# Carving setup scratch out of residual buffers, and rebalancing the setup engines, in a four-layer SSM/convolution kernel

## Chip, cores, metric

The kernel runs on one core of one Trainium2 chip. The metric is the device time of one execution in microseconds (us); lower is better. Engines are named as the profile names them: PE (TensorE, matrix products), PEld (its weight loads), DVE (VectorE), ACT (ScalarE), POOL (GpSimd), SP (SyncE, which issues most of the DMAs here).

The timings of one kernel spread by 1 to 2% with the granted TensorE clock. A few runs (one of `after_w3`, one each of `merged_w4`, `merged_late_w4` and `arena_late_w3`) are marked slow. The ratios leave these runs out; the medians quoted are of all runs, and differences are taken from the ratios. The rounds of experiments ran on different chips, each together with the kernel before, which is another reason to compare by ratio. Stage times are each read from one profiled execution, so a stage difference of a few us is not resolved by them.

## The reference, cut to what matters

```python
# x: [1, 2048, 640].  Four layers, each after a layernorm, each added to x:
x = x + A(layernorm(x))      # state-space layer: h_t = Lam_bar*h_{t-1} + B_bar x_t ; y = 2 Re(C h) + D x
x = x + Bl(layernorm(x))     # y = q * longconv(v * shiftconv(k)), q = layernorm(x)
x = x + A(layernorm(x))      # same weights again
x = x + Bl(layernorm(x))
# in Bl: k_shift = 4-tap causal convolution of k; kv = k_shift * v
#        y = irfft(rfft(kv, 4096) * rfft(ssm_k, 4096))[:2048] + kv * ssm_D
```

The long convolution doesn't depend on `x`. The kernel computes it once, as a side stream beside the first SSM layer, and both B layers only multiply by the result.

## The kernel before

The rows of `x` are cut into 16 chunks of 128. Each engine has its own instruction list; a scheduler lays out the lists when the kernel is built, so the order on an engine can differ from the source's. The kernel has two phases.

**Phase one** is the first SSM layer of all chunks, in four interleaved streams, with the FFT convolution as side stream. A round takes `FFT_W` steps of the FFT and then one step of each SSM stream:

```python
FFT_W = 3
NS1, NS2 = 4, 5
EVAC_DVE_EVERY = dict(T=2, F1=0, F2=4, I2=3, I1=2)   # every n-th PSUM eviction of a stage goes to DVE, 0: all to ACT

def run_streams(streams, side=None, side_w=1000, steps_per_chunk=None):
    ...
    while any(alive) or side is not None:
        if side is not None:
            for _ in range(side_w):
                next(side)                 # (StopIteration handled: cut)
        for i in reversed(range(n)):
            if alive[i] and rnd >= i:
                next(streams[i])           # (cut)
        rnd += 1
```

**An SSM chunk** goes x → T (transpose) → U (product with B) → P (two elementwise products) → G (prefix sums and carry) → H → Y → `xres`:

```python
    psT = ps("T", [P, D], BF16)                                   # PE transposes, ACT evicts to xT
    ...
    psU = ps("U", [P, D2], F32)                                   # 15 matmuls, L213
    ...
    U = wk.tile([P, D2], BF16, name="U", tag="uh")
    nc.scalar.copy(out=U[:], in_=psU[:])                          # L215
    yield
    P01 = wk.tile([P, D2], BF16, name="P01", tag="pa"); P23 = wk.tile([P, D2], BF16, name="P23", tag="pb")
    nc.vector.tensor_mul(out=P01[:], in0=U[:], in1=K["Wm2"][:])   # L218
    nc.vector.tensor_mul(out=P23[:], in0=U[:], in1=K["Wm2s"][:])  # L219
    yield
    psG = ps("G", [P, NB + 2, P], F32)
    ...
        nc.vector.scalar_tensor_tensor(out=x_dst, in0=psY[:], ..., in1=resid, ...)   # L274, writes xres[k]
```

In phase one T, U and G of every chunk share **one** PSUM buffer, since the FFT holds three banks.

```python
            if nm == "G" and "G" in pools:            # only in phase two
                return pools["G"].tile(shape, dt, name="ps_G", tag="G")
            if nm in ("T", "U", "G"):
                return psU.tile(shape, dt, name="ps_" + nm, tag="U")     # bufs=1
```

The buffer goes from use to use in the order of PE's list. In the trace of the kernel before, the first uses are T of chunks 0 and 1, U of chunk 0 (88.8 us), T of 2, U of 1 (96.3), T of 3, U of 2 (106.5), and only then the first G (110.7). So a use whose input is late holds back all uses behind it, those of other chunks too. T needs the chunk's layernorm (`xb`, after short DVE operations), U needs T, and G needs P.

**The side stream** prepares XB (a 40 KB-per-partition array), then transforms it:

```python
    XB = xbp.tile([P, 16, 2, D], BF16, name="XB")
    TF1 = make_TF1(tc, xbp, T)                        # DFT table; its temporaries in a pool of its own
    ...
        for dt in range(NT):
            ks = kp.tile([P, S], BF16, name="ksm", tag="ksm")
            nc.sync.dma_start(out=ks[:], in_=B_ssm_k[dt * P:(dt + 1) * P, :])
            nc.vector.tensor_add(out=ks[:, 0:1], in0=ks[:, 0:1], in1=dD[:, dt:dt + 1])
            ...                                        # 16 transposes (L539), 4 evictions into XB ("T")
    ...
    nc.sync.dma_start(out=XB[:, :, 0, :], in_=kview)  # 2.6 MB
    nc.vector.memset(hal[0:1, :, :], 0.0)             # L550
    ...
            nc.vector.tensor_copy(out=wj[:, j, :], in_=wsh[:, :, j])     # L559, four of them
    ...                                                # 4-tap convolution on DVE: L580 (product), L582 (sum), L583 (times v)
    TI1 = make_TI1(tc, tip, T)                        # tables for the inverse transform
    make_CS(tc, env["fconst"], T)                     # sines and cosines
    ...                                                # F1 (L600): first DFT -> DRAM; F2, pointwise, I2 (L666) -> DRAM; I1 (L686) -> ybuf
```

**Phase two** is the other three layers, in nine streams, with its own PSUM buffer for G. It starts after both streams of phase one are through:

```python
        run_streams(g1, side=gf, side_w=FFT_W, steps_per_chunk=7)
    pools["G"] = ctx.enter_context(tc.tile_pool(name="psumG", bufs=1, space=PSUM))
    ...
    run_streams(gens, steps_per_chunk=8)
```

## Time and profile before

| | before |
|---|---|
| time, median of 3 runs (range) | 587.6 us (587.23 to 588.56) |
| span in the profile, mean granted clock | 586.2 us, 0.876 |
| PE / DVE / ACT busy | 417.0 / 414.0 / 336.0 us (71 / 71 / 57%) |
| transposes of the filter | 62 to 85 us |
| convolution on DVE | 88 to 164 us |
| first DFT (F1) done | 186.7 us |
| last DFT (I1) done | 391.9 us |
| last SSM chunk of phase one done | 394.8 us |
| first ps_U matmul of phase two | 411.0 us |

No engine is full on average, so the reading goes by stages. The first view is busy time by windows: each row is a stretch of the span in us, its length, the busy time and instruction count of each engine, the granted TensorE clock, the DMA share and GB/s.

```profile
...
core 0: us, PE busy (x) PEld busy (x) DVE busy (x) ACT busy (x) POOL busy (x), PEclk, DMA share, GB/s
...
30.00:60.00 30.00, 1.41 (x10) 0.91 (x10) 25.79 (x65) 7.34 (x12) 4.65 (x1) 0.50 0.30 91
60.00:90.00 30.00, 14.36 (x94) 10.46 (x95) 9.08 (x23) 7.25 (x12) 0.00 (x0) 0.50 0.31 101
90.00:120.00 30.00, 21.62 (x101) 9.66 (x100) 24.83 (x36) 17.60 (x34) 1.64 (x3) 0.84 0.32 113
...
390.00:420.00 30.00, 11.95 (x74) 6.39 (x73) 15.15 (x74) 24.88 (x54) 4.77 (x9) 0.72 0.21 72
...
```

PE has 1.41 us of work in 30 to 60, which is an empty setup; and in 390 to 420 again only 11.95 of 30. What PE waited for in the setup is seen from the transposes of the filter (one line's instructions: how many, their durations in ns, first and last start, then what ended the idle time before them):

```profile
...
L539 PE MATMUL ps_T<-identb,ksm x80: 265/314/314, 62.1 to 85.0; 128*128 128x128 bf16 x80
...
  DVE ksm L535: 13.2, 1
...
```

They could start only at 62.1, and the first of them waited for the filter's own load. The DMA issuer's waits between 40 and 65 us tell why that load was late:

```profile
...
SPq L549 <- DVE WmT L107: 22.9, 1, 22.9
SPq L531 <- DVE TF L484: 7.4, 1, 7.4
...
```

XB's load (L549) waited 22.9 us for a table computation (WmT), and the first load of the filter's stage (L531, just ahead of the filter's tiles L534 on the same queue) 7.4 us for the last write of the DFT table. Neither load needs the result that it waited for. They lay in the same SBUF bytes: the temporary pools had been closed and the new tiles took their place. Then follows the convolution (the products that start an accumulation),

```profile
...
L580 DVE TENSOR_TENSOR acc<-XB,wj x7: 483/818/824, 88.3 to 147.6; 128x1280 bf16<-128x1280 bf16 x6, 128x640 bf16<-128x640 bf16 x1
...
```

from 88.3 us on. At the other end, the timeline of PE shows the change of phase (start, duration, engine, line, operation; in brackets the idle time before it and its releaser):

```profile
...
394.46 0.22 PE L269 MATMUL ps_Y<-DS,xT 128*128 128x128 bf16 x1
405.62 0.71 PE L204 MATMUL ps_T<-identb,xb 128*128 128x128 bf16 x5 [10.94 <-ACT xb L200]
...
411.03 4.31 PE L213 MATMUL ps_U<-BT,xT 128*128 128x512 bf16 x15 [1.39 <-ACT xT L206]
```

After the last matmul of phase one (394.5) PE is idle for 11 us and the first useful product of phase two starts at 411.0. Both streams had ended almost together (391.9 and 394.8), so `ybuf` had to be reloaded and a B layer computed with nothing else to do.

### The profile page before, as it was taken

The page shows a single profiled execution, that of the slowest core. Times are in us where ns is not written, and L with a number is a line of the kernel's source. Part 1 is how long each engine was busy: PE and PEld are TensorE (multiplying, and loading weights), DVE is VectorE, ACT ScalarE, POOL GpSimd, SP SyncE. Part 2 cuts the span into 40 slices and gives each one's busy share as a digit, 9 for nine tenths or more (in the row PEclk, how much of TensorE's full clock was granted, in tenths as well). Part 3 has the DMA queues.
Part 4 walks back from the last instruction along what each step waited for, and adds up shares of the span by engine and source line. Part 5 has one row for each costly group of instructions (what it writes and reads, how often), then busy time and mean ns, then how long its engine had stood idle before and what let it go on. Part 6 is the DMA issues. An engine that isn't in the chain of part 4 may idle for free. (4 is left out here: it accounts for less than half of the span.)

```text
span 586.2 us, 7978 instructions
## 1 busy us (share of the span) xinstructions
PE 417.0 (71%) x2814; PEld 225.2 (38%) x2814; DVE 414.0 (71%) x1126; ACT 336.0 (57%) x583; POOL 40.2 (7%) x81
## 2 busy tenths in 40 slices
PE   3300357689774789779898975990679898989981
PEld 3300233334332345334444432550335554545540
DVE  3798136998996297666888653665566888896883
ACT  2640122865868435555645652567965788965552
POOL 4003000000010000000000000003000101100001
PEclk9655557978878899989999997995889999999997
DMA  7305321444522441664563228123000101010000
GB/s 256 104 0 178 124 83 27 181 158 172 210 102 73 118 102 38 143 142 107 122 152 96 68 67 358 79 104 101 1 1 1 46 25 46 23 34 12 23 24 35
DMA packets 26791, 54.76 MB, mean 93 GB/s; under 512 B 6143, under 2 KB 14847, under 8 KB 26494
## 3 DMA queue, kind: packets, MB, share of 16 engines
q1 hardware_dynamic: 23806, 43.76, 25.0%
q0 software_dynamic: 2944, 10.49, 5.7%
q8 instruction: 22, 0.36, 0.3%
q14 instruction: 19, 0.16, 0.1%
HBM read 33.26 MB, written 20.97 MB: 93 GB/s over the span
## 5 line engine op out<-in xcount | busy, mean ns | idle before, releaser
L213 PE MATMUL ps_U<-BT,xT 128*128 128x512 bf16 (+1 forms) x480 | 106.1, 375 | 20.3 <-ACT xT L206 19.5
L266 PE MATMUL ps_Y<-CT,H 128*128 128x128 bf16 (+1 forms) x640 | 107.9, 307 | 8.5 <-DVE xres L274 6.5
L213 PEld LDWEIGHTS <-xT 128*128 128x128 bf16 x480 | 49.6, 105 | 68.6 <-issue 38.3
L215 ACT CAST U<-ps_U 128x1280 bf16<-128x1280 f32 x32 | 39.1, 1222 | 58.5 <-PE ps_U L213 58.4
L266 PEld LDWEIGHTS <-H 128*128 128x128 bf16 x640 | 49.2, 99 | 44.1 <-issue 12.5
L238 ACT CAST G<-ps_G 128x1280 bf16<-128x1280 f32 x32 | 39.2, 1225 | 34.5 <-PE ps_G L236 27.5
L233 PE MATMUL ps_G<-Lpos,P 128*128 128x128 bf16 x320 | 47.2, 221 | 7.8 <-ACT U L215 6.3
L218 DVE TENSOR_TENSOR P<-U,Wm 128x1280 bf16<-128x1280 bf16 x32 | 26.3, 820 | 32.8 <-ACT U L215 32.8
L519 ACT CAST s<-ps_F 128x512 bf16<-128x512 f32 (+1 forms) x96 | 42.2, 553 | 7.7 <-PE ps_F L600 7.6
L175 ACT ACTIVATE ln_junk<-xres 128x640 bf16<-128x640 f32 x48 | 35.0, 730 | 13.2 <-DVE c L247 4.7
L519 ACT CAST XS<-ps_F 128x512 bf16<-128x512 f32 (+1 forms) x70 | 36.5, 578 | 5.5 <-PE ps_F L639 5.0
L233 PEld LDWEIGHTS <-P 128*128 128x128 bf16 x320 | 29.8, 97 | 19.0 <-issue 13.7
L600 PE MATMUL ps_F<-XB,TF 128*128 128x512 bf16 (+1 forms) x96 | 29.9, 376 | 10.0 <-ACT s L519 5.4
L204 PE MATMUL ps_T<-identb,xb 128*128 128x128 bf16 x160 | 15.5, 233 | 29.3 <-ACT xb L200 18.9
L234 PEld LDWEIGHTS <-P 128*128 128x128 bf16 x320 | 31.3, 98 | 10.0 <-issue 7.8
L206 ACT COPY xT<-ps_T 128x640 bf16<-128x640 bf16 x32 | 22.2, 694 | 17.9 <-PE ps_T L204 17.9
L638 PE MATMUL ps_F<-a2in,F_C 128*128 128x512 bf16 (+1 forms) x76 | 29.5, 388 | 3.4 <-DVE a2o L517 2.5
L236 PE MATMUL ps_G<-E,cT 20*128 20x512 bf16 (+1 forms) x90 | 31.4, 349 | 0.0
L285 ACT ACTIVATE bq<-xres,ln_nb,ln_rstd 128x640 bf16<-128x640 f32 x32 | 28.6, 916 | 4.2 <-DVE ln_nb L188 4.1
L539 PE MATMUL ps_T<-identb,ksm 128*128 128x128 bf16 x80 | 11.7, 302 | 24.7 <-DVE ksm L535 13.2
L219 DVE TENSOR_TENSOR P<-U,Wm2s 128x1280 bf16<-128x1280 bf16 x32 | 26.1, 815 | 0.4 <-ACT U L215 0.4
L255 DVE TENSOR_TENSOR M<-G,TA 128x1280 bf16<-128x1280 bf16 x32 | 26.1, 816 | 0.0
(256 smaller groups left out, 809.7 us busy)
## 6 DMA issues: line engine op xcount, KB each, us to landing
Ad<-s SPq DMA_DIRECT2D x32, 320.0 KB, 2.2
a2in<-Ad SPq DMA_DIRECT2D x28, 320.0 KB, 5.1
AIN<-ad SPq DMA_DIRECT2D x2, 2560.0 KB, 12.0
ad<-a2o SPq DMA_DIRECT2D x28, 160.0 KB, 2.6
xin<-in_A_x_dram POOLq DMA_DIRECT2D x16, 160.0 KB, 2.9
vb<-in_B_v_dram POOLq DMA_DIRECT2D x8, 320.0 KB, 3.3
XB<-in_B_k_dram SPq DMA_DIRECT2D x1, 2560.0 KB, 10.5
ksm<-in_B_ssm_k_dram SPq DMA_DIRECT2D x5, 512.0 KB, 3.4
```

The costliest lines, as they stand in the source:

```text
L175: nc.scalar.activation(out=junk[:], in_=x_ap, func=ACTF.Square, accum_out=ssq[:])
L213: nc.tensor.matmul(out=psU[:, c0:c1], lhsT=xT[:, dt * P:(dt + 1) * P], rhs=BTf[:, dt, c0:c1], start=dt == 0, stop=dt == NT - 1)
L215: nc.scalar.copy(out=U[:], in_=psU[:])
L233: nc.tensor.matmul(out=psG[:, b, :], lhsT=src[:, pt * P:(pt + 1) * P], rhs=Lpos[:], start=b == b0, stop=False)
L234: nc.tensor.matmul(out=psG[:, b, :], lhsT=src[:, D + pt * P:D + (pt + 1) * P], rhs=sgn[:], start=False, stop=lastmm)
L236: nc.tensor.matmul(out=psG[:, b0:b0 + nb_, :], lhsT=cT[:], rhs=K["E2"][:, b0:b0 + nb_, :], start=False, stop=True)
L238: nc.scalar.copy(out=G[:].rearrange("p r t j -> p (r t) j"), in_=psG[:, 0:NB, :])
L266: nc.tensor.matmul(out=psY[:, c0:c1], lhsT=H[:, hi, pt, :], rhs=CT[:, pt, hi, c0:c1], start=n == 0, stop=False)
L285: nc.scalar.activation(out=q[:], in_=x, func=ACTF.Identity, bias=nb[:, 0:1], scale=rstd[:, 0:1])
L519: nc.scalar.copy(out=out, in_=in_)
L600: nc.tensor.matmul(out=pt_[:, :c1 - c0], lhsT=TF1[:, r, mh, :], rhs=XBf[:, r, c0:c1], start=True, stop=True)
L638: nc.tensor.matmul(out=pt_[:, :c1 - c0], lhsT=C[:], rhs=a2f[:, ro, c0:c1], start=True, stop=False)
```

## The change

The intent: temporaries of the setup go into the tiles of the residual `xres`, which are written late (chunks 2 to 8 and 9 to 15), so that XB, the filter tiles and the inverse table no longer overlap them in memory. Weight loads use working tiles of the SSM streams. Some setup work moves from DVE to POOL, the evictions of the transposes all go to ACT, and the FFT gets four steps in a round in place of three.

```diff
+class Arena:                    # hands out pieces of one SBUF tile; release(mark) frees them
+    ...
-    es = ExitStack(); tp = es.enter_context(tc.tile_pool(name="tbl_tmp", bufs=1))
+                                # build_tables, fft_tables, make_CS, make_TF1, make_TI1 take an arena `tp` instead
 ...
-            w = wl.tile([P, NT, D], BF16, name="wsb", tag="wsb")
-            nc.sync.dma_start(out=w[:], in_=src.rearrange("(t p) d -> p t d", p=P))
+            for (t0, t1, tag) in parts:                      # ((0,2,"pa"), (2,4,"pb"), (4,NT,"uh"))
+                w = wk.tile([P, 2, D], BF16, name="wsb", tag=tag)
+                nc.sync.dma_start(out=w[:, 0:t1 - t0, :], in_=sv[:, t0:t1, :])
 ...
-    TF1 = make_TF1(tc, xbp, T)
+    TF1 = make_TF1(tc, xbp, T, env["arena2"])
 ...
-            nc.vector.tensor_add(out=ks[:, 0:1], in0=ks[:, 0:1], in1=dD[:, dt:dt + 1])
+            nc.gpsimd.tensor_add(out=ks[:, 0:1], in0=ks[:, 0:1], in1=dD[:, dt:dt + 1])
 ...
-    nc.vector.memset(hal[0:1, :, :], 0.0)
+    nc.gpsimd.memset(hal[0:1, :, :], 0.0)
 ...
-            nc.vector.tensor_copy(out=wj[:, j, :], in_=wsh[:, :, j])
+            nc.gpsimd.tensor_copy(out=wj[:, j, :], in_=wsh[:, :, j])
 ...
-    TI1 = make_TI1(tc, tip, T)
-    make_CS(tc, env["fconst"], T)
+    ar2 = env["arena2"]
+    ar2.release(0)
+    TI1 = make_TI1(tc, tip, T, ar2)
+    make_CS(tc, env["fconst"], T, ar2)
 ...
-FFT_W = 3
+FFT_W = 4
-EVAC_DVE_EVERY = dict(T=2, F1=0, F2=4, I2=3, I1=2)
+EVAC_DVE_EVERY = dict(T=0, F1=0, F2=4, I2=3, I1=2)
 ...
-    xres = [const.tile([P, D], F32, name=f"xres{k}") for k in range(nch)]
+    xres_all = const.tile([P, nch, D], F32, name="xres")
+    xres = [xres_all[:, k, :] for k in range(nch)]
+    arena = Arena(xres_all[:, 2:9, :].rearrange("p k d -> p (k d)"))
+    arena2 = Arena(xres_all[:, 9:nch, :].rearrange("p k d -> p (k d)"))
```

(The same replacement is made in each table function.)

More of the change, by code (lines that the diff above doesn't have):

```diff
@@ L13, with __init__, mark, release @@
 PI = math.pi
+class Arena:
+    def __init__(self, ap):
+        self.ap = ap; self.off = 0; self.tags = {}
+    def mark(self):
+        return self.off
+    def release(self, mark):
+        self.off = mark
+        self.tags = {k: v for k, v in self.tags.items() if v[0] < mark}
+    def tile(self, shape, dtype, name=None, tag=None):
+        n = 1
+        for s_ in shape[1:]:
+            n *= s_
+        esz = mybir.dt.size(dtype)
+        nw = (n * esz + 3) // 4
+        nw = (nw + 7) // 8 * 8
+        if tag is not None and tag in self.tags:
+            off, have = self.tags[tag]
+            assert have >= nw, (tag, have, nw)
+        else:
+            off = self.off; self.off += nw
+            assert self.off <= self.ap.shape[1], ("arena overflow", name, self.off, self.ap.shape)
+            if tag is not None:
+                self.tags[tag] = (off, nw)
+        v = self.ap[0:shape[0], off:off + nw]
+        if dtype != F32:
+            v = v.bitcast(dtype)
+        v = v[:, 0:n]
+        if len(shape) > 2:
+            names = [f"d{i}" for i in range(len(shape) - 1)]
+            v = v.rearrange(f"p ({' '.join(names)}) -> p {' '.join(names)}", **{nm_: s_ for nm_, s_ in zip(names[1:], shape[2:])})
+        return v
 def _sincos(nc, pool, ang, shape, negpi, tag):
@@ L30, in _sincos, with build_tables @@
     return outs[0], outs[1]
-def build_tables(ctx, tc, const, psum_tile, identb, negpi, A_Lambda_re, A_Lambda_im, A_log_dt):
+def build_tables(ctx, tc, const, tp, psum_tile, identb, negpi, A_Lambda_re, A_Lambda_im, A_log_dt):
     nc = tc.nc
     D = A_Lambda_re.shape[0]; NT = D // P
-    es = ExitStack(); tp = es.enter_context(tc.tile_pool(name="tbl_tmp", bufs=1))
     cols = []
@@ L114, in build_tables, with load_weightsT @@
         nc.vector.tensor_copy(out=Wm2s[:, (1 - ri) * D:(2 - ri) * D], in_=ps[:])
-    es.close()
     return dict(TA=TA, TB=TB, LL=LL, LI=LI, Wm2=Wm2, Wm2s=Wm2s, negpi=negpi)
-def load_weightsT(ctx, tc, const, psum_tile, identb, A_B_re, A_B_im, A_C_re, A_C_im):
+def load_weightsT(ctx, tc, const, wk, psum_tile, identb, A_B_re, A_B_im, A_C_re, A_C_im):
     nc = tc.nc
     D = A_B_re.shape[0]; NT = D // P
-    es = ExitStack(); wl = es.enter_context(tc.tile_pool(name="wload", bufs=2))
     n_ev = [0]
@@ L125, in load_weightsT @@
     CT = const.tile([P, NT, 2, D], BF16, name="CT")
+    parts = ((0, 2, "pa"), (2, 4, "pb"), (4, NT, "uh"))
     for dst, srcs in ((BT, (A_B_re, A_B_im)), (CT, (A_C_re, A_C_im))):
         for ri, src in enumerate(srcs):
-            w = wl.tile([P, NT, D], BF16, name="wsb", tag="wsb")
-            nc.sync.dma_start(out=w[:], in_=src.rearrange("(t p) d -> p t d", p=P))
+            sv = src.rearrange("(t p) d -> p t d", p=P)
+            wrow = {}
+            for (t0, t1, tag) in parts:
+                w = wk.tile([P, 2, D], BF16, name="wsb", tag=tag)
+                nc.sync.dma_start(out=w[:, 0:t1 - t0, :], in_=sv[:, t0:t1, :])
+                for rt in range(t0, t1):
+                    wrow[rt] = w[:, rt - t0, :]
             for ct in range(NT):
@@ L132, in load_weightsT @@
                 for rt in range(NT):
-                    nc.tensor.transpose(out=ps[:, rt * P:(rt + 1) * P], in_=w[:, rt, ct * P:(ct + 1) * P], identity=identb[:])
+                    nc.tensor.transpose(out=ps[:, rt * P:(rt + 1) * P], in_=wrow[rt][:, ct * P:(ct + 1) * P], identity=identb[:])
                 n_ev[0] += 1
@@ L138, in load_weightsT @@
                     nc.vector.tensor_copy(out=dst[:, ct, ri, :], in_=ps[:])
-    es.close()
     return BT, CT
@@ L299, in setup_early, with setup_consts @@
     return dict(identb=identb, negpi=negpi)
-def setup_consts(ctx, tc, const, psum_tile, K0, A_Lambda_re, A_Lambda_im, A_B_re, A_B_im, A_C_re, A_C_im, A_log_dt, A_Dskip):
+def setup_consts(ctx, tc, const, arena, wk, psum_tile, K0, A_Lambda_re, A_Lambda_im, A_B_re, A_B_im, A_C_re, A_C_im, A_log_dt, A_Dskip):
     nc = tc.nc
@@ L305, in setup_consts @@
     identb = K0["identb"]
-    BT, CT = load_weightsT(ctx, tc, const, psum_tile, identb, A_B_re, A_B_im, A_C_re, A_C_im)
-    K = build_tables(ctx, tc, const, psum_tile, identb, K0["negpi"], A_Lambda_re, A_Lambda_im, A_log_dt)
+    BT, CT = load_weightsT(ctx, tc, const, wk, psum_tile, identb, A_B_re, A_B_im, A_C_re, A_C_im)
+    K = build_tables(ctx, tc, const, arena, psum_tile, identb, K0["negpi"], A_Lambda_re, A_Lambda_im, A_log_dt)
     K["identb"] = identb
@@ L406, in _sin_table, with fft_tables @@
     nc.scalar.activation(out=out, in_=r[:], func=ACTF.Sin, bias=negpi[: shape[0], 0:1], scale=2 * PI / 4096.0)
-def fft_tables(ctx, tc, const, negpi):
+def fft_tables(ctx, tc, const, tp, negpi):
     nc = tc.nc
-    es = ExitStack(); tp = es.enter_context(tc.tile_pool(name="ftbl_tmp", bufs=1))
     T = {"negpi": negpi}
@@ L441, in fft_tables, with make_CS @@
     T["fk"], T["isq1"], T["offk"], T["wa"] = fk, isq1, offk, wa
-    es.close()
     return T
-def make_CS(tc, const, T):
+def make_CS(tc, const, T, tp):
     nc = tc.nc
-    with tc.tile_pool(name="fcs_tmp", bufs=1) as tp:
+    if True:
         pidx = tp.tile([P, 1], I32, name="pidx"); nc.gpsimd.iota(pidx[:], pattern=[[0, 1]], base=0, channel_multiplier=1)
@@ L462, in make_CS, with make_TF1 @@
             T[nm] = t
-def make_TF1(tc, pool, T):
+def make_TF1(tc, pool, T, tp):
     nc = tc.nc
-    with tc.tile_pool(name="tf1_tmp", bufs=1) as tp:
+    if True:
         tt = tp.tile([P, 16, NQ], I32, name="tt"); nc.gpsimd.iota(tt[:], pattern=[[1, 16], [0, NQ]], base=0, channel_multiplier=16)
@@ L485, in make_TF1, with make_TI1 @@
     return TF1
-def make_TI1(tc, pool, T):
+def make_TI1(tc, pool, T, tp):
     nc = tc.nc
@@ L491, in make_TI1 @@
     nc.gpsimd.memset(TI1[:], 0.0)
-    with tc.tile_pool(name="ti1_tmp", bufs=1) as tp:
+    if True:
         ti = tp.tile([P, 16, 2, 16], I32, name="ti"); nc.gpsimd.iota(ti[:], pattern=[[1, 16], [64, 2], [128, 16]], base=0, channel_multiplier=0)
@@ L733 @@
     fconst = ctx.enter_context(tc.tile_pool(name="fconst", bufs=1))
-    T = fft_tables(ctx, tc, fconst, K0["negpi"])
+    T = fft_tables(ctx, tc, fconst, arena, K0["negpi"])
     wk1 = ctx.enter_context(tc.tile_pool(name="wk1", bufs=NS1)); io1 = ctx.enter_context(tc.tile_pool(name="io1", bufs=NS1))
@@ L737 @@
         pools["F"] = c1.enter_context(tc.tile_pool(name="psumF", bufs=3, space=PSUM))
-        envF = mk_env(None, None, evac_dve_every=EVAC_DVE_EVERY, fconst=fconst)
+        envF = mk_env(None, None, evac_dve_every=EVAC_DVE_EVERY, fconst=fconst, arena2=arena2)
         gf = fft_conv(c1, tc, envF, T, K0["identb"], B_k, B_v, B_shift_k, B_ssm_k, B_ssm_D, Ad[:], ad[:], ybuf[:])
@@ L741 @@
             next(gf)
-        K = setup_consts(ctx, tc, const, lambda nm, shape, dt: pools["F"].tile(shape, dt, name="ps_w", tag="F"), K0,
+        K = setup_consts(ctx, tc, const, arena, wk1, lambda nm, shape, dt: pools["F"].tile(shape, dt, name="ps_w", tag="F"), K0,
                          A_Lambda_re, A_Lambda_im, A_B_re, A_B_im, A_C_re, A_C_im, A_log_dt, A_Dskip)
```

## The prediction

> **What bounds the kernel now.** The span is 586.2 us; PE and DVE are busy 71%, ACT 57%. No engine is full, so I read stages (busy time by windows, timeline).
>
> 1. Setup, 0 to 88 us. PE is busy 10.6 us in 0–30, 1.4 in 30–60, 14.4 in 60–90. The cause is memory reuse: the transposes of the filter (L539) start only at 62 us, because XB, TI1 and ksm lie where the temporary pools of tables and weights lay. XB's load is issued at 49.0 us, right after the last table transposes (48.1), the first ksm load at 57.6, right after the last TF1 write (57.1). The 20 groups of transposes take 62–85 us, 1.18 us each, serial through one PSUM buffer. The shift convolution (L580) begins at 88.35, and x's first transposes wait behind L539 in PE's order until 85.8.
> 2. 88–191: convolution and first DFT; DVE is 90% busy or more until 170.
> 3. 200–348: second and inverse DFT; 348–393: reload and last DFT. The phase-one SSM chunks run beside them and end at 394.8.
> 4. Change of phase: PE busy 1.4 us in 400–410; the first phase-two ps_U matmul is at 411.0, since both streams end together and ybuf must be reloaded first.
>
> **What the change does.** Arithmetic stays. Scratch moves into residual tiles that are written late, so XB, ksm and TI1 no longer wait for tables. Weight loads become 12, all issued early. Five 0.16 us ksm additions, the hal memset (0.86 us) and four wj copies (1.62 us in all) go from DVE to POOL; ten evictions (0.42 us on DVE) become 0.59 us on ACT. FFT_W 3 to 4 gives the FFT more steps per round.
>
> By the instruction order, ksm transposes now follow the weight transposes directly. But all table and TF1 work on DVE still stands before the first L580 product: about 42 us net of overlap by the trace's durations, most of it after the Lambda loads, which now queue behind the weight loads (estimate: landing at 16–20 us). So I estimate the convolution's start at 57 us (50–66), 30 us earlier.
>
> The Trainium skill (SBUF — State Buffer, Who interferes with whom) says DVE and GpSimd share a port pair as an exclusive lock. The copies on POOL may stretch; I allow 1–2 us each. They end near 53 us by my estimate, so a slow POOL costs little unless it passes 60.
>
> Then: first DFT done at 135 (some SSM work is pushed later), second stage 148–273, last DFT done at 310. With FFT_W 3 both streams need about 31 rounds; with 4 the FFT needs 23. So four SSM chunks stay alone at the end, about 50 us, since T, U and G of a chunk share one PSUM buffer. Phase one ends near 360. In that tail ybuf is ready, so the first phase-two ps_U comes about 2 us later, not 16. Phase two keeps its order and its 175 us, perhaps 5 less.
>
> Sum: 30 (setup) + 5 (stages) + 14 (change of phase) + 5 = about 53 us, hence **535 us**, range 515 to 558. Faster by over 2%: 0.94; within 2%: 0.05; slower: 0.01.
>
> **What would show it.** L580's first product at 50–66 us; ksm transposes from about 22; first DFT done by 145; phase-two ps_U before 370, with no 10 us hole on PE before it; ahead of it 40 us or more of SSM alone; 2814 matmuls.
>
> **What would make it wrong.** XB's 2.6 MB load delaying the later ksm loads; POOL copies blocked; ACT overfull at 60–135 us (evictions of 49 us plus SSM); an SSM tail longer than 50 us.

## The result, and the profile after

| | before | after |
|---|---|---|
| median on the same chip (range) | 586.13 us (582.14 to 589.8, 15 runs) | **563.39 us** (559.59 to 565.31, 12 runs) |
| ratio, 95% interval | | **0.9598** [0.9568, 0.9628] |
| span, clock in the profile | 586.2 us, 0.876 | 562.0 us, 0.877 |
| transposes of the filter | 62 to 85 | 21.5 to 48 |
| convolution on DVE | 88 to 164 | 55 to 118 |
| F1 done | 186.7 | 146.2 |
| second stage (I2) done | 347.4 | 286.2 |
| I1 done | 391.9 | 326.3 |
| last SSM chunk of phase one done | 394.8 | 389.1 |
| first ps_U of phase two | 411.0 | 388.5 |

Ratios here and below are the mean time of a kernel's fast runs over the mean of the kernel before's fast runs of the same rounds, so not quite the ratio of the medians quoted.

It is 4% faster. The prediction said 535 us, with a range of 515 to 558: the time lies above the range. The FFT ends 66 us earlier; the SSM stream, which runs beside it, ends 6 us earlier. In the changed kernel the lines have other numbers: the filter's transposes L539 are L576 there, the convolution's products L580 are L617, F1 L600 is L639, ps_U L213 is L252, U's eviction L215 is L254, P L218 and L219 are L257 and L258, and `xres` L274 is L313. The windows answer to those of before:

```profile
...
30.00:60.00 30.00, 10.84 (x76) 8.06 (x76) 27.91 (x64) 15.45 (x25) 9.99 (x12) 0.50 0.24 77
60.00:90.00 30.00, 20.77 (x59) 6.70 (x59) 30.00 (x55) 21.85 (x51) 2.18 (x4) 0.61 0.51 179
90.00:120.00 30.00, 22.49 (x96) 8.85 (x95) 28.23 (x54) 22.92 (x48) 1.08 (x2) 0.67 0.42 155
...
390.00:420.00 30.00, 21.85 (x148) 11.83 (x147) 18.74 (x63) 22.26 (x39) 0.54 (x1) 0.94 0.02 7
...
```

(Columns as above.) "Done" for a chunk is the start of its last write of `xres`, 0.8 us long. The hole in the setup is smaller (PE 10.84 in 30 to 60) and so is that at the change of phase (21.85 in 390 to 420). DVE is now full from 60 to 120, 30.00 and 28.23 of 30. The transposes and the convolution come where the prediction had put them:

```profile
...
L576 PE MATMUL ps_T<-identb,ksm x80: 217/311/333, 21.5 to 47.7; 128*128 128x128 bf16 x80
...
  POOL ksm L572: 4.5, 4
...
```

```profile
...
L617 DVE TENSOR_TENSOR acc<-XB,wj x7: 484/818/827, 54.8 to 102.6; 128x1280 bf16<-128x1280 bf16 x6, 128x640 bf16<-128x640 bf16 x1
...
```

The change of phase and the last `xres` of phase one, on PE and on DVE; first DVE before, then DVE after, then PE after:

```profile
...
394.77 0.82 DVE L274 SCALAR_TENSOR_TENSOR xres<-ps_Y,xin 128x640 f32<-128x640 f32 x1
...
```

```profile
...
389.09 0.82 DVE L313 SCALAR_TENSOR_TENSOR xres<-ps_Y,xin 128x640 f32<-128x640 f32 x1
...
```

```profile
...
388.45 0.22 PE L308 MATMUL ps_Y<-DS,xT 128*128 128x128 bf16 x1
388.51 2.87 PE L252 MATMUL ps_U<-BT,xT 128*128 128x512 bf16 x15
...
```

The product of phase two follows the last of phase one with no gap. So the 24.2 us of the two spans split into three: the end of phase one moved by 5.7 (394.8 to 389.1), the interval from there to the first ps_U shrank by 16.8 (from +16.3 to −0.6), and phase two itself (first ps_U to the end) by 1.7 (175.2 to 173.5).

The puzzle is the first of these. Everything that the setup won is visible in the FFT, but the SSM stream's end hardly moved.

### The profile page after: what moved, and what is told of

Its sections match the earlier page's. It is cut to its first block, busy times and chain, and to the rows that moved or that the text cites. A ratio compares the mean times of both kernels' runs of the same rounds, so it can differ in the third digit from the quotient of the medians.

```text
span 562.0 us, 7974 instructions
## 1 busy us (share of the span) xinstructions
PE 425.4 (76%) x2814; PEld 226.9 (40%) x2814; DVE 407.2 (72%) x1106; ACT 332.2 (59%) x585; POOL 48.9 (9%) x91
## 5 line engine op out<-in xcount | busy, mean ns | idle before, releaser
L252 PE MATMUL ps_U<-BT,xT 128*128 128x512 bf16 (+1 forms) x480 | 109.5, 379 | 16.4 <-ACT xT L245 15.6
L305 PE MATMUL ps_Y<-CT,H 128*128 128x128 bf16 (+1 forms) x640 | 106.2, 305 | 12.5 <-DVE xres L313 10.6
L252 PEld LDWEIGHTS <-xT 128*128 128x128 bf16 x480 | 50.0, 106 | 66.1 <-issue 35.6
L254 ACT CAST U<-ps_U 128x1280 bf16<-128x1280 f32 x32 | 39.1, 1223 | 46.1 <-PE ps_U L252 46.0
L257 DVE TENSOR_TENSOR P<-U,Wm 128x1280 bf16<-128x1280 bf16 x32 | 26.2, 820 | 30.9 <-ACT U L254 30.9
L639 PE MATMUL ps_F<-XB,TF 128*128 128x512 bf16 (+1 forms) x96 | 35.6, 462 | 13.9 <-DVE XB L620 11.0
L243 PE MATMUL ps_T<-identb,xb 128*128 128x128 bf16 x160 | 15.5, 233 | 26.5 <-ACT xb L239 13.0
L411 POOL DMA_DIRECT2D xin<-in_A_x_dram x16 | 8.8, 550 | 223.9 <-DVE ct L282 95.9
L191 DVE BATCH_NORM_STATS2 ln_st<-xin 128x6 f32<-128x320 bf16 x32 | 14.7, 479 | 18.5 <-DMA xin<-in_A_x_dram 18.5
L258 DVE TENSOR_TENSOR P<-U,Wm2s 128x1280 bf16<-128x1280 bf16 x32 | 26.1, 816 | 0.7 <-ACT U L254 0.7
```

The costliest lines, as they stand in the source:

```text
L252: nc.tensor.matmul(out=psU[:, c0:c1], lhsT=xT[:, dt * P:(dt + 1) * P], rhs=BTf[:, dt, c0:c1], start=dt == 0, stop=dt == NT - 1)
L305: nc.tensor.matmul(out=psY[:, c0:c1], lhsT=H[:, hi, pt, :], rhs=CT[:, pt, hi, c0:c1], start=n == 0, stop=False)
L639: nc.tensor.matmul(out=pt_[:, :c1 - c0], lhsT=TF1[:, r, mh, :], rhs=XBf[:, r, c0:c1], start=True, stop=True)
```

## The experiments

All variants but `two_taps` compute the reference's result. Milestones that recur, each from one profiled execution, in us:

| run | convolution starts | first SSM group (chunks 0 to 3) done | F1 done | I1 done | phase one's last chunk done | first ps_U of phase two | ratio to before |
|---|---|---|---|---|---|---|---|
| before | 88 | 177 | 187 | 392 | 394.8 | 411.0 | 1 |
| before_w4 | 88 | 183 | 184 | 361 | 420.9 | 420.3 | 1.0217 |
| arena_w3 | 72 | 158 | 162 | 366 | 369.3 | 384.8 | 0.9580 |
| arena_w4 | 71 | 154 | 155 | 328 | 387.3 | 386.8 | 0.9597 |
| after_w3 (second look) | 55 | 161 | 130 | 365 | 368.1 | 383.9 | 0.9596 |
| after | 55 | 161 | 146 | 326 | 389.1 | 388.5 | 0.9598 |
| late_w3 | 54 | 140 | 154 | 354 | 356.8 | 372.9 | 0.9465 |
| late_w4 | 55 | 149 | 149 | 320 | 380.0 | 379.4 | 0.9561 |
| arena_late_w3 | 73 | 158 | 162 | 363 | 365.8 | 381.5 | 0.9499 |
| two_taps | 55 | 147 | 148 | 320 | 379.5 | 378.9 | 0.9509 |
| tail_g | 55 | 159 | 145 | 324 | 378.4 | 383.0 | 0.9448 |

### 1. Which part of the change gives the 4%? `after_w3`, `before_w4`, `arena_w4`, `arena_w3`

The first theory was that `FFT_W` 4 was the mistake, because it strands four SSM chunks behind the FFT. The change was taken apart both ways: with and without `FFT_W` 4, with and without the moves between engines.

```diff
 # after_w3: the changed kernel with
-FFT_W = 4
+FFT_W = 3
 # before_w4: the kernel before with
-FFT_W = 3
+FFT_W = 4
 # arena_w4: the changed kernel with DVE and ACT work put back (arena_w3: the same with FFT_W = 3)
-            nc.gpsimd.tensor_add(out=ks[:, 0:1], ...)
+            nc.vector.tensor_add(out=ks[:, 0:1], ...)
-    nc.gpsimd.memset(hal[0:1, :, :], 0.0)
+    nc.vector.memset(hal[0:1, :, :], 0.0)
-            nc.gpsimd.tensor_copy(out=wj[:, j, :], in_=wsh[:, :, j])
+            nc.vector.tensor_copy(out=wj[:, j, :], in_=wsh[:, :, j])
-EVAC_DVE_EVERY = dict(T=0, F1=0, F2=4, I2=3, I1=2)
+EVAC_DVE_EVERY = dict(T=2, F1=0, F2=4, I2=3, I1=2)
```

Expected of `after_w3`:

> The changed kernel with FFT_W back at 3, all else kept. Theory 1 (the 33 us won in the setup went to the FFT stream, which FFT_W 4 then lets run ahead, so that four SSM chunks stand alone for 60 us): both streams end together again near 360 us, a hole of some 16 us follows, time 548 to 558, faster than the changed kernel (563). Rival (FFT_W 4 is what makes the gain, by closing the hole before phase two): 565 to 585, slower than the changed kernel.

Expected of `before_w4`:

> The kernel before with FFT_W 4 alone. Theory 1: FFT ends some 20 to 30 us earlier than 392, the last four SSM chunks stand alone, the hole before phase two closes; net within 2% of before, 575 to 595. Rival (FFT_W 4 is the gain): 560 to 572.

Expected of `arena_w4`:

> The changed kernel with the ksm additions, hal memset, wj copies and half of the transposed evictions back on DVE; arenas and FFT_W 4 kept. Theory 1 (the engine moves are off the path that ends last): the convolution starts 1 to 5 us later, time within 1% of the changed kernel, 558 to 569. Rival (the moved work counts, DVE being full from 50 to 110 us): 570 to 580.

Expected of `arena_w3`:

> Arenas alone: engines and FFT_W as before. Theory 1: nearly the whole setup gain arrives at the end, 550 to 562. Rival: 570 to 585.

Measured, medians and ratios with 95% intervals (before: 585.2 us):

| | engine moves off | engine moves on |
|---|---|---|
| FFT_W 3 | arena_w3: 561.31, 0.9580 [0.9539, 0.9622] | after_w3: 562.35, 0.9596 [0.9547, 0.9644] |
| FFT_W 4 | arena_w4: 562.54, 0.9597 [0.9553, 0.9641] | after: 563.39, 0.9598 [0.9568, 0.9628] |

and `before_w4`: 597.06, 1.0217 [1.017, 1.0264].

The arenas alone give the whole gain. The moves between engines bring the convolution forward by another 17 us (72 to 55) and the time by nothing. `FFT_W` 4 doesn't matter on top of the arenas and costs 2.2% in the kernel before. So the first theory fell: with `FFT_W` 3 the changed kernel is no faster. Three expectations were missed: the time of `after_w3` lies in neither range, that of `before_w4` 2.1 us above the theory's, and in `arena_w4` the convolution starts 16 us later than in the changed kernel (71 against 55), not 1 to 5.

The milestones show what `FFT_W` 4 trades. From arena_w3 to arena_w4 phase one ends 18.0 us later (369.3 to 387.3), but the interval to phase two's first product goes from +15.5 to −0.5 us, since the last loads of `ybuf` and the first B layers are done beside the stranded chunks. Net 2.0 us at that product. In the kernel before the same step costs 26.1 at the end of phase one and returns 16.9.

The profile of `after_w3` fell in a slow execution (clock 0.696), so it was looked at once more:

> The same kernel as after_w3, whose profile fell in the slow state: one look for a trace in the fast state. By theory 2, with FFT_W 3 and the early convolution, first DFT and first four SSM chunks are both done only at 155 to 163 us, as in the arenas alone (162), and the SSM ends near 370, as there; time 560 to 565.

It came out at 560.9 us, in the middle of the fast runs; its milestones are the ones in the table. They show the second riddle: with the convolution 17 us earlier than in arena_w3, its first SSM group is done at 161, not earlier than 158, and its last at 368.1 against 369.3.

### 2. Is the sum of DVE's work the limit? `two_taps`

DVE is full from 60 to 120 us. The rival to a cause in the order of work was plainly too much of it. So half of the convolution was removed (two of four taps; the result is wrong, though the convolution's share of the output is so small that the comparison still passed).

```diff
-            for j in (3, 2, 1, 0):
+            for j in (3, 2):
```

> The changed kernel with two of the four taps of the shift convolution left out; the result is wrong on purpose. That takes some 31 products and sums of 0.74 us net off DVE, about 23 us, all in the first 120 us. Theory 2 (the start is bound by the sum of DVE's work, so what the arenas won is only DVE's idle time, and an earlier convolution just pushes the SSM's DVE work back): the first DFT and the first four SSM chunks are both done 15 to 23 us earlier, and 10 to 22 us of it arrive at the end: 541 to 553. Rival (the order of rounds or PE bounds it): 556 to 565.

Measured: 556.19 us, ratio 0.9509 [0.9441, 0.9578], against 0.9598 of the changed kernel. DVE's busy time fell from 407.2 to 385.3 us, and the convolution ended at 85 in place of 118 us. The views of the convolution's products and of the F1 matmuls in `two_taps`, then of the F1 matmuls in the changed kernel:

```profile
...
L617 DVE TENSOR_TENSOR acc<-XB,wj x7: 485/809/815, 54.5 to 79.7; 128x1280 bf16<-128x1280 bf16 x6, 128x640 bf16<-128x640 bf16 x1
...
```

```profile
...
L639 PE MATMUL ps_F<-XB,TF x95: 269/379/586, 58.4 to 148.1; 128*128 128x512 bf16 x63, 128*128 128x256 bf16 x32
...
```

```profile
...
L639 PE MATMUL ps_F<-XB,TF x96: 269/421/634, 64.1 to 145.9; 128*128 128x512 bf16 x64, 128*128 128x256 bf16 x32
...
```

The convolution is over 33 us earlier, and yet F1's last matmul starts at 148.1 (145.9 in the changed kernel). The first SSM group is done at 147 in place of 161, and 10 us of this are left at the end of phase one. So removing 22 us of DVE work gives 5 us by the ratios (7 by the medians; the two intervals just overlap), and the time lies in the range of the rival. DVE's load may be part of the story, but F1's end doesn't follow the convolution's.

### 3. Is it the one PSUM buffer in the tail? `tail_g`, and phase two beside the tail: `merged_w4`

After the FFT ends (326 us) four chunks remain alone until 389. The tail of the changed kernel by windows (columns as in the first view), and two lines of PE's timeline in it:

```profile
...
330.00:340.00 10.00, 6.17 (x35) 3.14 (x34) 7.31 (x34) 7.83 (x14) 3.19 (x6) 1.00 0.37 118
340.00:350.00 10.00, 5.83 (x20) 2.74 (x21) 4.51 (x18) 8.03 (x16) 0.00 (x0) 0.66 0.01 2
350.00:360.00 10.00, 5.59 (x32) 2.76 (x32) 5.49 (x18) 3.73 (x6) 0.00 (x0) 0.61 0.00 1
360.00:370.00 10.00, 8.63 (x42) 3.83 (x41) 4.19 (x10) 2.45 (x2) 0.00 (x0) 0.71 0.00 0
...
```

```profile
...
342.59 0.69 PE L243 MATMUL ps_T<-identb,xb 128*128 128x128 bf16 x5 [2.78 <-ACT U L254]
344.06 5.14 PE L252 MATMUL ps_U<-BT,xT 128*128 128x512 bf16 x15 [0.78 <-ACT xT L245]
...
```

From 340 to 360 us PE is busy 5.8 and 5.6 of 10 us, at a granted clock of 0.66 and 0.61. The product ps_U took 5.14 us here, and 2.87 at full clock at 388.5 (above). Ahead of it PE had been idle for 2.78 us, waiting for an ACT eviction of the buffer that T, U and G share.

In `tail_g`, the FFT's three PSUM banks are given back when the FFT ends, and G gets a buffer of its own for the remaining chunks. In `merged_w4` moreover the streams of phase two start there, beside the last four SSM chunks.

```diff
 # tail_g: in run_streams, at the StopIteration of the side stream
+                    if on_side_end is not None:
+                        on_side_end()
 ...
+        def fft_done():
+            c1.close()
+            pools["G"] = ctx.enter_context(tc.tile_pool(name="psumG", bufs=1, space=PSUM))
-        run_streams(g1, side=gf, side_w=FFT_W, steps_per_chunk=7)
-    pools["G"] = ctx.enter_context(tc.tile_pool(name="psumG", bufs=1, space=PSUM))
+        run_streams(g1, side=gf, side_w=FFT_W, steps_per_chunk=7, on_side_end=fft_done)
 # merged_w4: fft_done also opens the pools of phase two and returns its nine streams, which join the
 # live ones (round s0 + i for stream i); a stream of phase two that reuses a phase-one pool waits its turn
+            s0 = max(rnd + 1, 7 * (nch // NS1) + 1 - NS2)
+            ...
+        run_merged(g1, gf, FFT_W, fft_done)
```

> The changed kernel, but once the FFT is done its PSUM banks are given to ps_G, so that in the last SSM chunks G no longer shares a buffer with T and U. Theory 3 (the shared PSUM buffer is what makes the SSM tail 63 us instead of my 50): tail 45 to 55 us, time 550 to 558. Rival (the tail is the length of the chain through four chunks, with late x loads and a halved clock): tail 58 us or more, time 559 to 566.

Measured: 554.15 us, ratio 0.9448 [0.9399, 0.9497]. The last chunk of phase one is done 54.1 us after the FFT (324.3 to 378.4), against 62.8 (326.3 to 389.1) in the changed kernel. So giving G its own buffer shortens the tail by about 9 us. The granted clock rose with it (0.94 over this tail, 0.84 over that of the changed kernel), so the wait for the buffer and the clock have not been separated. At the first ps_U of phase two 5.5 us of it are left (383.0 against 388.5); phase two itself is 4.7 us shorter. Windows of the tail:

```profile
...
340.00:350.00 10.00, 6.61 (x39) 3.44 (x38) 6.56 (x19) 7.91 (x15) 0.00 (x0) 1.00 0.00 0
350.00:360.00 10.00, 8.10 (x47) 4.16 (x49) 7.02 (x24) 4.45 (x5) 0.00 (x0) 0.67 0.00 1
...
```

From 340 to 350 PE is busy 6.61 at a full clock (5.83 and 0.66 in the changed kernel), from 350 to 360 8.10 (5.59).

> The changed kernel with both phases in one pool of streams: phase two begins when the FFT is done, beside the last four SSM chunks of phase one, with ps_G in the FFT's banks. If the tail of the SSM alone, with PE 56 to 60% busy, is where the gain went, filling it wins most of it back: 535 to 552, and the result stays right. Rival (DVE and ACT have no room there): 556 to 566.

Measured: 542.92 us, ratio 0.9233 [0.9149, 0.9318]; its interval lies clear of that of `tail_g`, run in the same rounds. Windows of the same stretch:

```profile
...
350.00:360.00 10.00, 8.80 (x63) 4.71 (x62) 7.91 (x25) 4.67 (x6) 0.00 (x0) 1.00 0.00 1
360.00:370.00 10.00, 9.07 (x80) 5.45 (x80) 6.85 (x23) 7.56 (x12) 0.54 (x1) 1.00 0.07 18
...
```

PE is busy 8.80 and 9.07 of 10 us from 350 to 370, at full clock. The tail isn't shorter (the last chunk of phase one is done at 392), but it no longer stands alone. This kernel beats both the kernel before and the changed one.

### 4. Why does the earlier convolution not reach the SSM stream? `late_w4`, `late_w3`, `arena_late_w3`

Back to the riddle of part 1. The SSM chunks run through one PSUM buffer, so one late use holds up the next chunks. The theory was that the first P products on DVE come too late. ACT's evictions of U of chunks 0 and 1 in the changed kernel, and DVE around the first P products:

```profile
...
68.64 1.28 ACT L254 CAST U<-ps_U 128x1280 bf16<-128x1280 f32 x1
...
111.27 1.23 ACT L254 CAST U<-ps_U 128x1280 bf16<-128x1280 f32 x1 [3.02 <-PE ps_U L252]
...
```

```profile
...
100.00 0.82 DVE L258 TENSOR_TENSOR P<-U,Wm2s 128x1280 bf16<-128x1280 bf16 x1
...
105.90 0.82 DVE L257 TENSOR_TENSOR P<-U,Wm 128x1280 bf16<-128x1280 bf16 x1
...
```

U of chunk 0 is in SBUF at 69.9 us, but its P products start at 100.0 and 105.9. There is no idle time before them: on DVE they stand behind 24 and 28 products of the convolution (L617) and behind the tables `TI1` and `make_CS`. The Trainium skill (TensorE: Matmul & The Clock Gate, Architectural detail: the array is 16× 32×32) says that the queues of ScalarE and VectorE are strictly in order. This trace agrees: an operand 30 us old didn't let P overtake. But P isn't what the buffer waited for. After U of chunk 0 its next uses are T of chunk 2 and then U of chunk 1, and T of chunk 2 waited for that chunk's layernorm, whose last DVE operation (L201) stands behind 27 of the same products. The end of the layernorm on DVE, then T of chunk 2 and the first G on PE:

```profile
...
103.87 0.15 DVE L201 SCALAR_TENSOR_TENSOR ln_nb<-ln_mvb,ln_rstd 128x1 f32<-128x1 bf16 x1
...
```

```profile
...
105.55 0.71 PE L243 MATMUL ps_T<-identb,xb 128*128 128x128 bf16 x5 [0.24 <-ACT xb L239]
...
118.08 0.22 PE L272 MATMUL ps_G<-Lpos,P 128*128 128x128 bf16 x1 [0.77 <-ACT U L254]
...
```

Hence U of chunk 1 only at 111.3. The first G, at 118.1, was released by an eviction of U; the P that it reads had been done since 106.7. With `FFT_W` 3 (`after_w3_again`) it is the layernorm of chunk 3, further on, that ends late, behind 31 products; again DVE, then PE:

```profile
...
109.80 0.15 DVE L201 SCALAR_TENSOR_TENSOR ln_nb<-ln_mvb,ln_rstd 128x1 f32<-128x1 bf16 x1
...
```

```profile
...
111.06 0.71 PE L243 MATMUL ps_T<-identb,xb 128*128 128x128 bf16 x5 [0.23 <-ACT xb L239]
...
```

Its first G starts at 117.4. In `arena_w3`, where the convolution starts 17 us later, the layernorms of all four chunks are through at 63.2, before the convolution, and the first P products stand behind its first three products. U's evictions, then the last layernorm and the first P on DVE:

```profile
...
77.90 1.23 ACT L254 CAST U<-ps_U 128x1280 bf16<-128x1280 f32 x1 [5.43 <-PE ps_U L252]
...
84.98 1.23 ACT L254 CAST U<-ps_U 128x1280 bf16<-128x1280 f32 x1 [4.64 <-PE ps_U L252]
...
```

```profile
...
63.08 0.16 DVE L201 SCALAR_TENSOR_TENSOR ln_nb<-ln_mvb,ln_rstd 128x1 f32<-128x1 bf16 x1
...
79.16 0.83 DVE L257 TENSOR_TENSOR P<-U,Wm 128x1280 bf16<-128x1280 bf16 x1 [3.68 <-ACT U L254]
...
```

The eviction of its second U starts at 85.0, 26 us earlier than in the changed kernel, and its first G at 94.8, 22.6 us earlier than in `after_w3_again`. It looks as though the setup, running ahead, let more of DVE's gap-filling work be laid ahead of the layernorms and of P. If so, moving the tables out of the way should bring them forward. Only the place of the two table functions changes:

```diff
-    ar2 = env["arena2"]
-    ar2.release(0)
-    TI1 = make_TI1(tc, tip, T, ar2)
-    make_CS(tc, env["fconst"], T, ar2)
-    C, Sn, NS = T["C"], T["S"], T["NS"]
     XBf = XB[:].rearrange("p r s d -> p r (s d)")
     ...                                              # F1 loop over rb = 15 .. 0
+            if rb == 8:
+                ar2 = env["arena2"]
+                ar2.release(0)
+                TI1 = make_TI1(tc, tip, T, ar2)
+                make_CS(tc, env["fconst"], T, ar2)
+                C, Sn, NS = T["C"], T["S"], T["NS"]
```

> The changed kernel with the table building that fills gaps (inverse tables and cosine/sine tables) moved out of the convolution and into the middle of the first DFT; nothing else. Theory 4 (VectorE's order makes the first SSM group late: U evacuated at 69 us, its P only at 100): the P of chunk 0 comes 10 to 20 us earlier, the first group of x residuals is done at 142 to 155 us (161 in the changed kernel), the last group moves by the same, and the time is 545 to 557. Rival (the second to fourth groups are set by the FFT's evictions and DMA, whatever the first group does): first group earlier but the last group still ends at 385 to 391, time 559 to 566.

> The same with FFT_W 3. Theory 4: first group done at 142 to 155, last DFT done and SSM end near 355 to 365, first phase-two U near 378, time 550 to 558. Rival: as the changed kernel with FFT_W 3 (560 to 564).

Measured: `late_w3` 553.32 us, ratio 0.9465 [0.9394, 0.9535]; `late_w4` 560.92 us, ratio 0.9561 [0.9495, 0.9628].

The last layernorm of the first group and the first P products on DVE in `late_w3` (P stands behind 6 and 8 products of the convolution), and the last `xres` of the first group, in `late_w3` and then in `after_w3_again`:

```profile
...
64.51 0.14 DVE L201 SCALAR_TENSOR_TENSOR ln_nb<-ln_mvb,ln_rstd 128x1 f32<-128x1 bf16 x1
...
66.64 0.83 DVE L258 TENSOR_TENSOR P<-U,Wm2s 128x1280 bf16<-128x1280 bf16 x1 [1.99 <-ACT U L254]
...
```

```profile
...
140.28 0.82 DVE L313 SCALAR_TENSOR_TENSOR xres<-ps_Y,xin 128x640 f32<-128x640 f32 x1
...
```

```profile
...
160.94 0.77 DVE L313 SCALAR_TENSOR_TENSOR xres<-ps_Y,xin 128x640 f32<-128x640 f32 x1
...
```

With `FFT_W` 3 the first group is done 20.7 us earlier (140.3 against 160.9), the last chunk of phase one 11.3 earlier (356.8 against 368.1), and the ratio falls from 0.9596 to 0.9465, by intervals that do not meet. The first G starts at 85.0 in place of 117.4. So the order of DVE is shown as the cause there; that it acts through the layernorms more than through P is read from the waits of PE above, since the move brought both forward. The profiled run of `late_w3` was the fastest of its four (550.25 us, clock 0.915; `after_w3_again` 0.886), so part of its milestones may be the clock; the ratio is over all runs. With `FFT_W` 4 the first group moved by 12 us and the last chunk by 9 in the profile, but there too the profiled run was the fastest of its four, at a clock of 0.91, and the ratio's interval overlaps that of the changed kernel. There the theory's time (545 to 557) was missed: what becomes of those us beside the stranded tail is not settled.

The control puts the same move into the arenas alone, where P was early already:

```diff
 # arena_w3, with the move of late_w3
```

> The arenas alone with FFT_W 3 (engine moves undone, ksm transposes from 39 us, convolution from 72 us), with the table building moved as in the late-tables run. If VectorE's order is what hid the engine moves: here chunk 0's P was early already (U evacuated at 78, 85, 94 us), so little is won: first SSM group done at 148 to 158 us (158 without the move), time 556 to 562, 3 to 9 us above the run with engine moves and late tables (553.3). Rival (the late tables help by themselves, and the engine moves are worth nothing even so): first group at 140 to 145 us, time 550 to 555, equal to that run.

Measured: 558.06 us, ratio 0.9499 [0.9428, 0.957]. The first group is done at 158, as without the move: here the tables were not in its way. In fact the move hardly changed DVE's order: the products of `TI1` still run before the convolution (59.4 to 64.6 us; 56.9 to 62.1 in `arena_w3`), so this run is no test of late tables by themselves. By the profiles it stays 17 us behind `late_w3` in the first group, and 9 us behind at the end of phase one (365.8 against 356.8), against the fastest run of `late_w3`. The ratios differ by only 0.0034, about 2 us, in the expected direction (3 to 9 us were expected), and their intervals overlap. So what the engine moves are worth once the order is mended shows in the first group's milestone, and is not shown in the time.

### 5. Both together: `merged_late_w4`

```diff
 # merged_w4, with the move of late_w4
```

> Phase two started at the FFT's end beside the last four SSM chunks, with the table building moved as in the run of the late tables. If the first group's gain is carried on: 526 to 539 us (merged alone 542.9). If it is not carried, or the table building now delays the FFT: 540 to 548.

Measured: 542.49 us, ratio 0.922 [0.9144, 0.9295]: the same as `merged_w4`. The second of the two expectations held. The first SSM group is done 8 us earlier (152 against 160), but the first U of phase two is evicted at 361 against 360. Phase two's streams start at the FFT's end, which is about the same (323.9 against 325.5); that this is why nothing is carried on is argued, not shown.

## Why the prediction was wrong

Point by point:

- **Setup: right in its times, and half right in the cause.** Transposes from about 22: 21.5. Convolution at 57 (50 to 66): 54.8. But the arenas alone, which remove the memory reuse, start the transposes only at 39 us and the convolution at 71 to 72; the other 16 to 17 us of the 33 come from the engine moves, which the prediction counted as some 7 us of DVE work (by the durations in its text). The 4% of the time come from the arenas alone.
- **The loads to come late, POOL slow: harmless, as predicted.** The Trainium skill (SBUF — State Buffer, Who interferes with whom) says that the DVE/GpSimd port pair is an exclusive lock. The trace has one clear case that agrees: a copy on DVE (0.80 us in the kernel before) took 2.50 us, from 7.80 to 10.30, while a POOL memset ran from 6.09 to 9.62; so it ended 0.68 us after the memset, as if it had begun then. The copies of wj took 4.0 us on POOL and ended at 54.1 ("near 53" was predicted).
- **FFT: right in kind, late by 11 to 16 us.** F1 done at 146.2 against 135, I2 at 286.2 against 273, I1 at 326.3 against 310. F1's own size was fine; its remaining steps stand between SSM steps on PE (the last two matmuls start at 145.7 and 145.9, right behind a Y). `two_taps` showed that even an end of the convolution 33 us earlier leaves F1 at 148.
- **Change of phase: right.** It shrank by 16.8 us (14 was predicted), there is no hole ahead of the first ps_U, and four chunks stand alone before it.
- **Phase two:** 1.7 us less, where 5 was allowed.
- **The step that failed** is "So four SSM chunks stay alone at the end, about 50 us ... Phase one ends near 360". Phase one ended at 389.1. The 29 us are 16 from the FFT's end and 13 from the tail (62.8 against 50); the rest of the sum is within 4 us. The prediction made phase one's end the FFT's end plus a fixed tail, so that every us won in the setup passed on to it. The runs show something else. The end is that of the SSM stream, whose chunks follow each other through one PSUM buffer, and it can stay late when the FFT is early. The arenas bring its end forward by 25.5 us with `FFT_W` 3; the engine moves add nothing to it (368.1 against 369.3), because DVE's order then puts the layernorm of the fourth chunk behind the convolution (its end at 110.0 us, against 63.2 with the arenas alone), and the chunks wait for it at the buffer; and `FFT_W` 4 gives 21.0 us back (368.1 to 389.1), of which 16.4 return at the change of phase (the interval there goes from +15.8 to −0.6).
- **"What would make it wrong"** named "an SSM tail longer than 50 us", rightly. What it missed: the tail runs partly at a clock of 0.61 to 0.66, and its length includes about 9 us that a buffer of G's own removes (`tail_g`, where the clock rose too). The Trainium skill (TensorE: Matmul & The Clock Gate, Why this matters for your kernels) advises no idle gaps of over about 3 us between bursts of matmuls. In the trace the clock halved within a shorter gap: PE was idle for 2.78 us until 342.6, the granted clock reads 1.00 from 338 to 341.8 and 0.50 from 341.9 to 348.6, and ps_U then took 5.14 us, against 2.87 elsewhere. No run holds the clock alone, so its share of the 13 us is not separated from that of the waits.

What stays open: why `late_w4` keeps so little of its earlier first group, what part of the tail's extra length is the clock, and why the FFT's later stages add another 5 us to F1's delay of 11.

## What to carry to other kernels

Removing false memory dependences in the setup pays only as far as the stream that ends last is let through: follow the won time to the milestone that ends the phase, stream by stream, before adding it to the total. When one stream is moved earlier, look at the in-order engine that it shares with the other: work that used to fill gaps may now stand ahead of a short operation on which a one-buffer chain hangs. And where a phase ends in a tail of a few serial items, starting the next phase beside it (−20 us here) was worth more than any balance within the phase that was tried.

## What the Trainium skill lacked or had wrong

- GPSIMD Engine Reference, 3.1 Elementwise — side-by-side cycle accounting: the only measured ratio in that section is for an fp32 `tensor_tensor` add, 1.96 times slower than DVE. Here a strided bf16 copy of 128x640 took 1.04 us on POOL (mean of four, 0.74 to 1.24) against 0.458 on DVE, and the fill of one row 2.00 against 0.86, both 2.3 times; the two views are shown below, POOL in the changed kernel and DVE in the kernel before. DVE was at work beside both on POOL, so what the port lock adds to them is not known.

```profile
...
48.11 2.00 POOL L587 MEMSET hal<- 1x1920 bf16 x1 [6.90 <-PE ps_T L576]
50.07 4.00 POOL L596 COPY wj<-wsh 128x640 bf16<-128x640 bf16 x4
...
```

```profile
...
L559 DVE COPY wj<-wsh 128x640 bf16<-128x640 bf16 x4 | 1.6, 458 | 0.0
...
L550 DVE MEMSET hal<- 1x960 uint32 x1 | 0.9, 858 | 0.1
...
```

- TensorE: Matmul & The Clock Gate, Why this matters for your kernels: its row on gaps puts the limit at about 3 us. Here the clock halved within an idle stretch of 2.78 us, and the next ps_U took 5.14 us in place of 2.87.
- PSUM — Partial Sum Buffer has no price for one buffer shared by successive steps of a pipeline. Here it was about 9 us for four chunks (62.8 against 54.1 us), with the change of the granted clock that came with it.
- No page tells that moving independent work earlier can delay a dependent chain on an in-order engine. Here P products waited 30 us after their operand was ready (69.9 to 100.0 in the changed kernel), a layernorm ended at 110.0 us instead of 64.7 (`after_w3_again` against `late_w3`), and by the ratios this order cost about 8 us (0.9596 against 0.9465).
